# Float32 values without zero columns, weight chunks decoded in halves behind the heads, three query buffers and 20 constant products, in a windowed-attention and feed-forward kernel

## The chip, the cores and the metric

The kernel runs on one core of a Trainium2 chip. The metric is the device time of one execution in microseconds, as the median of several runs. The core has a matrix engine (TensorE, PE in the rows, with PEld for its weight loads), a vector engine (VectorE, DVE), a scalar engine (ScalarE, ACT), a general engine (GpSimd, POOL) and a queue engine that issues most DMAs (SyncE, SP; SPq is its instruction queue). Each engine works through its own instructions in a fixed order.

## The reference

There are 8 batches of 8 heads. Each head has 512 local tokens and 32 global ones, of 64 elements. A local query sees the 32 global keys and the local keys at most 32 positions away; a global query sees all keys. The attention's output, 4608 rows of 512, goes through a feed-forward layer of width 2048.

```python
s_g   = scale * q_g @ k_all.T;          out_g = softmax(s_g) @ v_all
s_ll  = where(abs(i - j) <= 32, scale * q_l @ k_l.T, -1e9)
a_l   = softmax(concat([scale * q_l @ k_g.T, s_ll]));   out_l = a_l @ v_all
x = concat([out_g, out_l]) as (4608, 512)
h = x @ w_in;  r = maximum(h, 0);  g = s * (r * r) + b;  out = g @ w_out
```

## The kernel before, in words

The work of a head is cut into two halves of 256 queries; one such half is called a head here, counted by `j` from 0 to 127. Eight heads (`j` = 8t to 8t+7) give one tile of 256 rows of x, and tile t of the feed-forward layer is worked in eight steps `m` = 8t to 8t+7, each with 24 products into `ps_h` (L517) and 12 into `acc` (L549). A 17th tile holds the global rows. Most operands are held as two parts, a rounded one and its remainder, so that the products are accurate; but the first NF = 16 heads use plain float32 operands, as their splitting would add to the start.

The loop over `j` (L602) traces, in this order: the loads of head j+2, the loads of weight chunks, the decoding of weight chunk `j` (only for j below 16), the scores of head `j`, the feed-forward step m = j - 10, the transposes of head j-1, the product with the values of head j-2 (`pv32`, L332, which works on two heads together when the second is due), the load of values, the split of a finished x tile (`x_split`, L484, at j = 9, 17, ...), and the second half of feed-forward step m-1.

**Weight chunks.** The weights of the feed-forward layer come as 16 chunks of 1 MB (`weight_load`, L139), each in two loads into a staging buffer. `weight_words` (L154) decodes a chunk into `w_all` with three ScalarE instructions (L160, L161, L168) and three VectorE instructions (L164, L165, L169), each over 1024 columns; the first two chunks (BY_HALVES = 2) are decoded in two halves of 512 columns. Step m needs chunks 2m and 2m+1. The staging buffers are those of the x tiles (xs0, xs1) and of the split queries and keys (kq).

**Float32 heads.** `load32` (L261) loads the queries `rq`, with zeros in the rows of the pair's other head, into one of two buffers in turn: the only `rq` buffer, or `tg`. `v_load32` (L274) loads values from `in_vz`, 192 KB a head: beside the head's 64 columns stand 64 columns of zeros, so that both heads of a pair add into the same 128 rows of `ps_o`. There are two `rv` buffers. `scores32` (L279) makes four constant products (`keep_busy`, L102) while j is below 10, then the scores, and for every second head the products of the global queries (L295); `softmax` (L217) has VectorE and ScalarE by turns.

**Order.** The instructions get a rank as they are traced. A planner hands each engine, at each step of its own estimate of time, the ready instruction that ranks first, and gives out buffers in the same way; so the order on each engine is fixed when the program is built. The functions of the first 16 heads are traced under

```python
with tc.high_priority(offset=AHEAD):
```

which ranks them AHEAD places earlier. AHEAD is 0. A DMA that needs a buffer waits in the SP queue for it, and what is behind it in that queue waits too. The 28 constant products at the start (WARM_FIRST, L107) give TensorE work while the first loads come. The loads of the scalars s and b (L566, L567) are the first two on the SP queue.

Of the kernel before, what the change touches and what calls it, by code (L numbers as in the profile page):

```python
# [10 lines left out]
F32 = mybir.dt.float32  # L11
# [9 lines left out]
B, H, SL, SG, D = 8, 8, 512, 32, 64  # L21
DM, DF = 512, 2048
P = 128
HALF = 256
# [16 lines left out]


NF = 16
AHEAD = 0


LAG = 10
SPLIT_AT = {8 * t + 9: t for t in range(16)}
WARM_UNTIL = 10
WARM_FIRST = 28  # L50
WARM_HEAD = 4

SPOTS = ["xs0", "xs1", "kq", "kq"] * 2 + ["xs1", "kq", "kq"] * 2 + ["xs1", "kq"]
LOADS_AT = {0: (0, 1), 1: (2, 3), **{j: (j + 2,) for j in range(2, 14)}}
BY_HALVES = 2
NORM_ACT = lambda j: j < 0
X_ACT = lambda j: j >= 8
G_AT = (13, 18)
# [9 lines left out]


@with_exitstack  # L70
def window_attention_then_ffn(ctx: ExitStack, tc: tile.TileContext, qd, qg, kw, vw, vg, qz, qgz, vz, w_in, w_out, sv, bv, out):
    nc = tc.nc
    scale = 1.0 / math.sqrt(D)

# [11 lines left out]
    sb = ctx.enter_context(tc.tile_pool(name="sb", bufs=2))  # L86
# [7 lines left out]
    s_t = const.tile([P, 1], F32, name="s_t")  # L94
    b_t = const.tile([P, 1], F32, name="b_t")
# [6 lines left out]
    def keep_busy(n, name):  # L102
        p_w = ps.tile([P, 512], F32, tag="acc1", name=name)
        for _ in range(n):
            nc.tensor.matmul(p_w, lhsT=warm[:, 0:P], rhs=warm, start=True, stop=True)

    keep_busy(WARM_FIRST, "warm0")  # L107


    for tile_, c0, shift in ((mask_low, 32, -32), (mask_mid, 32, 0), (mask_high, 0, 32)):  # L110
        nc.gpsimd.memset(tile_, 0.0)
        part = tile_[:, c0:c0 + 192]
        for sign, base in ((1, -shift), (-1, 64 + shift)):
            nc.gpsimd.affine_select(
                out=part, in_=part, pattern=[[sign, 192]], compare_op=ALU.is_ge,
# [23 lines left out]
    def weight_load(k):  # L139
        st = ops.tile([P, 2048], I32, tag=SPOTS[k], name=f"wst{k}", bufs=1 + (SPOTS[k] == "kq"))  # L140
        staged[k] = st
        sources = (w_in[k], w_out[k * P:(k + 1) * P, :])
        for i in range(2):
            queue = nc.scalar if k == 0 else nc.sync
            queue.dma_start(st[:, 1024 * i:1024 * (i + 1)], sources[i])

    def weight_chunk(k):
        st = staged.pop(k)
        n = 2 if k < BY_HALVES else 1
        for i in range(n):  # L150
            c = 1024 // n
            weight_words(k, st[:, 2 * c * i:2 * c * (i + 1)], slice(c * i, c * (i + 1)))

    def weight_words(k, st, at):  # L154
        words = st.rearrange("p (n w) -> p n w", w=2)
        low, high = words[:, :, 0], words[:, :, 1]
        n = at.stop - at.start
        pool, tag = ((ops, "vsg"), (sb, "pg"))[(k + at.start // 512) % 2]
        up = pool.tile([P, n], I32, tag=tag, name=f"wup{k}_{at.start}", bufs=1)
        nc.scalar.activation(out=up, in_=low.bitcast(U32), func=AF.Copy, scale=2.0**-29)  # L160
        nc.scalar.activation(  # L161
            out=low.bitcast(F32), in_=high.bitcast(F32), func=AF.Prelu, scale=2.0**-112, alpha=2.0**32,
        )
        nc.vector.tensor_scalar(out=low, in0=low, scalar1=3, scalar2=None, op0=ALU.logical_shift_left)  # L164
        nc.vector.tensor_tensor(out=low, in0=low, in1=up, op=ALU.add)  # L165
        m = low.bitcast(F32)
        hi, lo = (w_all[:, i, k].rearrange("p w c -> p (w c)")[:, at] for i in range(2))
        nc.scalar.copy(out=hi, in_=m)  # L168
        nc.vector.tensor_sub(out=lo, in0=m, in1=f32(hi))  # L169
# [3 lines left out]
    st_ = {}  # L173

    def slot(j):
        return j // 16, (j // 8) % 2, j % 8

    def load(j):
        b, hf, h = slot(j)
        if h % 2 == 0:  # L180
            rk = sb.tile([P, NK], F32, tag="rk", name=f"rk{j}", bufs=2)
            nc.sync.dma_start(rk, kw[b, hf, h // 2])
            st_["rk", j] = st_["rk", j + 1] = rk
        rq = sb.tile([P, HALF], F32, tag="rq", name=f"rq{j}", bufs=1)
        nc.sync.dma_start(rq, qd[b, hf, h])
        st_["rq", j] = rq

    def v_load(j):
        b, hf, h = slot(j)
        rv = sb.tile([P, 6 * D], F32, tag="rv", name=f"rv{j}")[:, 0:3 * D]  # L190
        nc.sync.dma_start(rv, vw[b, hf, h])
        st_["rv", j] = rv

# [60 lines left out]
    def x_tile(j):  # L254
        b, hf, h = slot(j)
        t = 2 * b + hf
        if h == 0:
            xcur[t] = sb.tile([P, 4, HALF], F32, tag="x", name=f"x{t}", bufs=1)
        return xcur[t]

    def load32(j):  # L261
        b, hf, h = slot(j)
        if h % 2 == 0:
            rk = sb.tile([P, NK], F32, tag="rk", name=f"rk{j}", bufs=2)
            nc.sync.dma_start(rk, kw[b, hf, h // 2])
            st_["rk", j] = st_["rk", j + 1] = rk
        if j % 2 == 0:
            rq = sb.tile([P, HALF], F32, tag="rq", name=f"rq{j}", bufs=1)
        else:
            rq = sb.tile([P, 288], F32, tag="tg", name=f"rq{j}", bufs=1)[:, 0:HALF]  # L270
        nc.sync.dma_start(rq, qz[j])
        st_["rq", j] = rq

    def v_load32(j):  # L274
        rv = sb.tile([P, 6 * D], F32, tag="rv", name=f"rv{j}")
        nc.sync.dma_start(rv, vz[j])
        st_["rv", j] = rv

    def scores32(j):  # L279
        b, hf, h = slot(j)  # L280
# [35 lines left out]
    def pieces(hf):  # L316
        q0 = MIDQ[hf][0]
        yield 0, P, slice(0, P), slice(0, P)
        yield 2, P, slice(NP - P, NP), slice(P, 2 * P)
        yield 1, MID, slice(P, NP - P), slice(q0, q0 + NP - 2 * P)  # L320
# [11 lines left out]
    def pv32(j):  # L332
        b, hf, h = slot(j)
        x = x_tile(j)
        if h % 2 == 0:
            return
        p_o = ps.tile([P, 2 * P], F32, tag="o", name=f"ps_o{j}")
        for i in (j - 1, j):
            pt, rv = st_.pop(("pt", i)), st_.pop(("rv", i))
            for c, n, o, q in pieces(hf):  # L340
                nc.tensor.matmul(  # L341
                    p_o[:, q], lhsT=rv[0:n, c * P:(c + 1) * P], rhs=pt[0:n, o],
                    start=(i < j and c == 0), stop=(i == j and c == 1),
                )
        x_out = x[:, h // 2, :]
        if X_ACT(j):
            nc.scalar.copy(out=x_out, in_=p_o)
        else:
            nc.vector.tensor_copy(out=x_out, in_=p_o)

    def qg_load(b):
        rqg = sb.tile([P, H * SG], F32, tag="xr", name=f"rqg{b}", bufs=1)
        nc.sync.dma_start(rqg, qgz[0] if b == 0 else qg[b])
        st_["rqg", b] = rqg

    def qg_load32(b):
        n = min(NF - 16 * b, H) * SG
        rqg = ops.tile([P, n], F32, tag="u", name=f"rqw{b}", bufs=1)
        nc.sync.dma_start(rqg, qgz[b, :, 0:n])
        st_["rqg", b] = rqg  # L360
# [202 lines left out]
                    rows = out.rearrange("(b r) d -> r b d", r=SL + SG)[16 * i:16 * i + 16, :, :]  # L563
                    nc.sync.dma_start(rows, o)

    nc.sync.dma_start(s_t, sv.partition_broadcast(P))  # L566
    nc.sync.dma_start(b_t, bv.partition_broadcast(P))  # L567

    NM = NT * 8
    extra, early, late = defaultdict(list), {}, {}  # L570
    for b in range(B):
# [10 lines left out]
    def pick(f32_one, split_one):  # L582
        def run(j):
            if NF <= j < NS:
                split_one(j)
            elif 0 <= j < NF:
                with tc.high_priority(offset=AHEAD):
                    f32_one(j)
        return run
# [5 lines left out]
    tr = pick(transposes32, lambda j: None)  # L595
    vsp = pick(lambda j: None, v_split)
    pvs = pick(pv32, lambda j: None)
    piece, last = 0, None
    qg_load(0)
    ld(0)  # L600
    ld(1)
    for j in range(NM + LAG + 2):  # L602
        sp(j + 1)
        ld(j + 2)
        vl(j)
        for k in LOADS_AT.get(j, ()):
            weight_load(k)
        if j < 16:
            weight_chunk(j)
            piece += 1  # L610
        if j < NS:
            b1 = j // 16 + 1
            if j == 14 and NF > 16:
                qg_load32(1)
            elif j % 16 == 14 and b1 < B:
                qg_load(b1)
            sc(j)
            if j == NF - 1 and NF % 16:
                if NF > 16:
                    qg_load(j // 16)  # L620
                qg_split(j // 16)
            if j % 16 == 15 and NF <= j + 1 < NS:
                qg_split(b1)
        if j in early:
            early.pop(j)()
        m = j - LAG if LAG <= j < NM + LAG else None
        if m is not None:
            ffn_in(m)
            if m == 8 * 15 + 7:
                xg_split(16)  # L630
        tr(j - 1)
        transposes_and_pv(j - 1, j - 2)
        vsp(j - 1)
        for fn in extra.pop(j, []):
            fn()
        pvs(j - 2)
        vl32(j)
        if j in SPLIT_AT:
            x_split(SPLIT_AT[j])
        if last is not None:  # L640
            ffn_out(last)
        last = m
        if j in late:
            late.pop(j)()
# [73 lines left out]
```

## Time and profile before

| | |
|---|---|
| median of 3 runs | 1037.92 us (1036.88 to 1038.34) |
| the profiled execution | 1040.1 us, span 1038.3 us |
| TensorE busy | 1008.4 us, 97% |
| VectorE busy | 793.1 us, 76% |
| ScalarE busy | 709.5 us, 68% |
| GpSimd busy | 282.1 us, 27% |
| moved by DMA | 82.05 MB |

The median is the time to compare with. The span is that of the instructions in the profiled execution, which was 1.8 us longer as a whole, and rows of the trace give times from the span's start. An engine is busy while it has an instruction in work. The constant products count as busy time of TensorE, though nothing reads them.

### The profile page before, as it was taken

To read this page: it belongs to the slowest core of one execution; us is meant where nothing else is said; L and a number is where in the kernel's file an instruction comes from. 1 tells how busy PE (TensorE), PEld (TensorE's weight loads), DVE (VectorE), ACT (ScalarE), POOL (GpSimd) and SP (SyncE) were. 2 spreads that over 40 slices of the span, in tenths; PEclk is the share of its full clock that TensorE was granted. 3 is DMA by queue.
4 is the path that set the end of the run, shared out by engine and by line. 5 is a ranking of instruction groups with operands and counts; after the bars stand their busy time and mean duration, and the time that the engine had idled before them with its cause. 6 is when DMAs were issued, how large, how long until landed. Compare 5 with 4: busy or idle time off the path is not lost.

```text
span 1038.3 us, 20034 instructions
## 1 busy us (share of the span) xinstructions
PE 1008.4 (97%) x6956; PEld 912.8 (88%) x6956; DVE 793.1 (76%) x2069; ACT 709.5 (68%) x1775; POOL 282.1 (27%) x366
## 2 busy tenths in 40 slices
PE   8669999999999999999999999999999999999998
PEld 4449999989999999999999999999999999999987
DVE  4888587788888888897779787898879787874322
ACT  6988576676777776786678686777678676754222
POOL 1001142333233242342243243332343233301000
PEclk9889999999999999999999999999999999999999
DMA  8774131321222121321123131222122122201000
GB/s 310 254 231 151 51 100 39 90 58 43 83 64 89 48 78 49 101 63 58 57 60 96 44 93 50 87 63 66 55 76 82 36 91 60 65 5 48 17 27 21
DMA packets 63558, 82.05 MB, mean 79 GB/s; under 512 B 7649, under 2 KB 50657, under 8 KB 63457
## 3 DMA queue, kind: packets, MB, share of 16 engines
q1 hardware_dynamic: 63168, 79.72, 25.0%
q8 instruction: 55, 0.90, 0.4%
q10 hardware_dynamic: 288, 1.05, 0.3%
q14 instruction: 47, 0.38, 0.1%
HBM read 71.30 MB, written 9.44 MB: 78 GB/s over the span
## 4 chain that ended last, share of the span: by engine, by line
PE 90%; DMA 3%; ACT 3%; DVE 3%; issue 1%; SPq 0%; DVEq 0%; ACTq 0%
PE ps_h L517 36%; PE acc L549 35%; PE ps_s L375 5%; PE ps_o L403 4%; PE turned L311 2%; PE turned L313 2%; PE ps_og L469 2%; PE ps_g L382 1%; DMA rk<-in_kw 1%; DMA wst<-in_w_in 1%; PE ps_o L341 1%; PE turned L447 1%; PE ps_s L286 1%; ACT wup L160 1%; ACT sm L231 1%
## 5 line engine op out<-in xcount | busy, mean ns | idle before, releaser
L517 PE MATMUL ps_h<-xst,w_all 128*128 128x256 f32 x3264 | 437.7, 281 | 2.7 <-ACT xst L489 1.8
L549 PE MATMUL acc<-w_all,g 128*128 128x512 f32 x1632 | 419.5, 396 | 0.0
L517 PEld LDWEIGHTS ps_h<-xst,w_all 128*128 128x128 f32 x3264 | 407.9, 189 | 10.0 <-ACT xst L489 2.0
L549 PEld LDWEIGHTS acc<-w_all,g 128*128 128x128 f32 x1632 | 291.2, 188 | 51.0
L231 ACT ACTIVATE sm<-sm,nm 128x224 f32<-128x224 f32 x256 | 121.5, 477 | 45.5 <-DVE nm L225 43.8
L524 DVE SCALAR_TENSOR_TENSOR r<-ps_h,s_t,r 128x512 f32<-128x512 f32 x136 | 101.4, 746 | 63.2 <-ACT r L523 62.2
L206 POOL TENSOR_TENSOR kq<-rq,kq 128x256 fp32r<-128x256 f32 x112 | 87.0, 777 | 203.1 <-ACT kq L205 188.5
L214 POOL TENSOR_TENSOR vs<-rv,vs 128x192 fp32r<-128x192 f32 x112 | 70.7, 631 | 259.9 <-ACT vs L213 253.6
L532 DVE SCALAR_TENSOR_TENSOR g<-r,b_t,g 128x512 fp32r<-128x512 f32 x136 | 108.4, 797 | 36.2 <-ACT g L531 32.3
L523 ACT ACTIVATE r<-ps_h 128x512 f32<-128x512 f32 x136 | 81.2, 597 | 75.3 <-PE ps_h L517 68.3
L531 ACT ACTIVATE g<-r,b_t 128x512 fp32r<-128x512 f32 x136 | 98.5, 724 | 37.4 <-DVE r L524 35.4
L241 DVE TENSOR_SCALAR sm<-sm,nm 128x224 f32<-128x224 f32 x256 | 83.1, 366 | 4.0
L461 POOL TENSOR_TENSOR vsg<-rvg,vsg 128x320 fp32r<-128x320 f32 x64 | 56.9, 911 | 105.2 <-ACT vsg L460 105.1
L375 PE MATMUL ps_s<-kq 128*128 128x224 f32 x448 | 75.0, 277 | 0.0
L375 PEld LDWEIGHTS ps_s<-kq 128*128 128x128 f32 x448 | 67.3, 190 | 6.4
L311 PE MATMUL turned<-ident,sm 128*96 128x128 f32 (+1 forms) x256 | 64.6, 277 | 6.3 <-DVE sm L241 6.3
L392 ACT CAST pt<-turned 128x416 fp32r<-128x416 f32 x112 | 57.5, 513 | 15.4 <-PE turned L313 14.5
L393 DVE TENSOR_TENSOR pt<-turned,pt 128x416 fp32r<-128x416 f32 x112 | 65.2, 583 | 2.8 <-ACT pt L392 2.0
L387 DVE TENSOR_TENSOR sg<-ps_g,tg 32x256 f32<-32x256 f32 (+1 forms) x112 | 48.2, 430 | 23.4 <-ACT tg L386 19.3
L403 PE MATMUL ps_o<-pt,vs 128*128 128x256 f32 x336 | 64.0, 296 | 0.1
L313 PE MATMUL turned<-ident,sm 128*128 128x128 f32 x256 | 63.8, 275 | 0.0
L204 POOL TENSOR_TENSOR kq<-rk,kq 64x352 fp32r<-64x352 f32 x56 | 60.2, 1074 | 10.5 <-ACT kq L203 5.1
(79 smaller groups left out, 1267.2 us busy)
## 6 DMA issues: line engine op xcount, KB each, us to landing
rq<-in_qd SPq DMA_DIRECT2D x112, 128.0 KB, 2.0
rk<-in_kw SPq DMA_DIRECT2D x64, 176.0 KB, 2.3
rv<-in_vw SPq DMA_DIRECT2D x112, 96.0 KB, 1.9
rvg<-in_vg SPq DMA_DIRECT2D x32, 320.0 KB, 3.0
out<-o SPq DMA_DIRECT2D x34, 256.0 KB, 2.1
wst<-in_w_in SPq DMA_DIRECT2D x15, 512.0 KB, 4.8
wst<-in_w_out SPq DMA_DIRECT2D x15, 512.0 KB, 5.7
rv<-in_vz SPq DMA_DIRECT2D x16, 192.0 KB, 3.5
```

The costliest lines, as they stand in the source:

```text
L206: nc.gpsimd.tensor_sub(out=qs[:, 1, :], in0=rq, in1=f32(qs[:, 0, :]))
L231: nc.scalar.activation(out=p, in_=p, func=AF.Exp, bias=nm[:, blk:blk + 1], scale=-1.0, accum_out=ss[:, blk:blk + 1],)
L241: nc.vector.tensor_scalar(out=p, in0=p, scalar1=ss[:, blk:blk + 1], scalar2=1.0, op0=ALU.mult, op1=ALU.mult,)
L311: nc.tensor.transpose(out=p_t[0:n, s0:s0 + P], in_=sm[:, c0:c0 + n], identity=ident)
L313: nc.tensor.transpose(out=p_t[:, o0:o0 + P], in_=sm[:, c0:c0 + P], identity=ident)
L375: nc.tensor.matmul(p_s[:, W * blk:W * blk + W], lhsT=qs[:, a, blk * P:(blk + 1) * P], rhs=ks[:, KEYS[blk]], start=(a == 0), stop=(a == 1),)
L403: nc.tensor.matmul(p_o[:, :, q], lhsT=vs[0:n, c], rhs=pt[0:n, :, o], start=(c == 0), stop=(c == 1))
L517: nc.tensor.matmul(p_h[:, k], lhsT=wi[:, a, f, c], rhs=xs[:, e, c, :], start=(n == 0), stop=(n == 11),)
L524: nc.vector.scalar_tensor_tensor(out=r, in0=p_h, scalar=s_t, in1=r, op0=ALU.mult, op1=ALU.mult)
L531: nc.scalar.activation(out=g[:, 0], in_=r, func=AF.Identity, bias=b_t)
L532: nc.vector.scalar_tensor_tensor(out=g[:, 1], in0=r, scalar=b_t, in1=f32(g[:, 0]), op0=ALU.add, op1=ALU.subtract,)
L549: nc.tensor.matmul(oacc[t][i], lhsT=g[:, a, k, i * P:(i + 1) * P], rhs=wo[:, e, f, :], start=(pr == 0 and n == 0), stop=(pr == 7 and n == 5),)
```

## The change

Values: `vz` is gone. The first 16 heads load their values as all others do (`v_load`, 96 KB), into one of three `rv` buffers of half the size. `pv32` multiplies with 64 stationary columns and writes the 64 rows of `ps_o` that belong to the head, each head with its own start and stop. Queries: `rq` has two buffers, and the float32 heads go through three in turn (`rq`, `rq`, `tg`). Chunks: all 16 are decoded in halves, so every chunk takes six ScalarE and six VectorE instructions of 512 columns; the traced place of loads and decodings stays but for chunk 2, which is loaded at j = 0. Order: the functions of the first 16 heads rank 50 places earlier. Start: 20 constant products in place of 28, and the loads of s and b are traced at j = 3.

```diff
-AHEAD = 0
+AHEAD = 50
-WARM_FIRST = 28
+WARM_FIRST = 20
-LOADS_AT = {0: (0, 1), 1: (2, 3), **{j: (j + 2,) for j in range(2, 14)}}
-BY_HALVES = 2
+DECODED_AT = [0, 1, 2, 3, 4, 5, 6, 7, 8, 9, 10, 11, 12, 13, 14, 15]
+BY_HALVES = 16
...
-        rq = sb.tile([P, HALF], F32, tag="rq", name=f"rq{j}", bufs=1)
+        rq = sb.tile([P, HALF], F32, tag="rq", name=f"rq{j}", bufs=2)
...
-        rv = sb.tile([P, 6 * D], F32, tag="rv", name=f"rv{j}")[:, 0:3 * D]
+        rv = sb.tile([P, 3 * D], F32, tag="rv", name=f"rv{j}", bufs=3)
...
-        if j % 2 == 0:
-            rq = sb.tile([P, HALF], F32, tag="rq", name=f"rq{j}", bufs=1)
+        if j % 3 < 2:
+            rq = sb.tile([P, HALF], F32, tag="rq", name=f"rq{j}", bufs=2)
...
     def v_load32(j):
-        rv = sb.tile([P, 6 * D], F32, tag="rv", name=f"rv{j}")
-        nc.sync.dma_start(rv, vz[j])
-        st_["rv", j] = rv
+        v_load(j)
...
             for c, n, o, q in pieces(hf):
+                d0 = D * (i % 2)
                 nc.tensor.matmul(
-                    p_o[:, q], lhsT=rv[0:n, c * P:(c + 1) * P], rhs=pt[0:n, o],
-                    start=(i < j and c == 0), stop=(i == j and c == 1),
+                    p_o[d0:d0 + D, q], lhsT=rv[0:n, c * D:(c + 1) * D], rhs=pt[0:n, o], start=(c == 0), stop=(c == 1),
                 )
...
-    nc.sync.dma_start(s_t, sv.partition_broadcast(P))
-    nc.sync.dma_start(b_t, bv.partition_broadcast(P))
...
     for j in range(NM + LAG + 2):
+        if j == 3:
+            nc.sync.dma_start(s_t, sv.partition_broadcast(P))
+            nc.sync.dma_start(b_t, bv.partition_broadcast(P))
         sp(j + 1)
         ld(j + 2)
         vl(j)
-        for k in LOADS_AT.get(j, ()):
-            weight_load(k)
-        if j < 16:
-            weight_chunk(j)
+        while loaded < 16 and (loaded < 2 or DECODED_AT[loaded] <= j + 2):
+            weight_load(loaded)
+            loaded += 1
+        while piece < 16 and DECODED_AT[piece] <= j:
+            weight_chunk(piece)
             piece += 1
```

## Rows read from the trace of the kernel before

**Rows 1.** Stages: length, busy PE, PEld, DVE, ACT, POOL, PE clock, DMA share, GB/s.

```profile
0.00:10.36 10.36, 8.91 (x28) 3.31 (x28) 1.61 (x3) 4.16 (x7) 3.19 (x15) 1.00 0.59 202
10.36:80.89 70.53, 49.31 (x223) 33.45 (x223) 57.51 (x146) 61.43 (x110) 0.00 (x0) 0.86 0.80 273
80.89:119.40 38.51, 38.51 (x261) 35.60 (x260) 29.18 (x67) 27.89 (x62) 8.64 (x9) 0.98 0.35 109
119.40:1000.00 880.60, 878.00 (x6244) 810.53 (x6243) 695.98 (x1844) 607.50 (x1586) 270.25 (x342) 1.00 0.22 63
```

**Rows 2.** Timeline of PE: start, length, instruction; idle time before it and what ended it.

```profile
14.80 0.65 PE L295 MATMUL ps_g<-rk,rqg 128*64 128x256 f32 x2 [1.97 <-ACT sg L300]
15.38 1.02 PE L286 MATMUL ps_s<-rk,rq 128*128 128x224 f32 x4
...
39.58 1.70 PE L286 MATMUL ps_s<-rk,rq 128*128 128x224 f32 x4
...
54.66 0.99 PE L295 MATMUL ps_g<-rk,rqg 128*64 128x288 f32 x2 [2.56 <-DMA rk<-in_kw]
...
65.84 0.47 PE L311 MATMUL turned<-ident,sm 128*128 128x128 f32 x1 [3.44 <-DVE sm L241]
...
74.27 0.89 PE L341 MATMUL ps_o<-pt,rv 128*128 128x128 f32 x6
...
80.89 4.92 PE L517 MATMUL ps_h<-xst,w_all 128*128 128x256 f32 x34
```

**Rows 3.** Timeline of ACT and DVE at the end of the start.

```profile
71.82 1.14 ACT L160 ACTIVATE wup<-wst 128x1024 int32<-128x1024 uint32 x1 [0.64 <-DMA wst<-in_w_out]
...
73.33 0.42 DVE L349 COPY x<-ps_o 128x256 f32<-128x256 f32 x1
...
76.29 0.61 ACT L489 CAST xst<-x 128x512 fp32r<-128x512 f32 x1
```

**Rows 4.** What the SP queue waited for from 10.36 to 80.89: total, times, longest.

```profile
SPq L276 <- PE ps_o L341: 18.0, 10, 5.6
SPq L271 <- PE ps_s L286: 9.3, 9, 2.3
SPq L145 <- DVE w_all L169: 8.7, 5, 4.7
```

**Rows 5.** ACT in the same stretch by line and shape: busy, mean ns, idle before.

```profile
L160 ACT ACTIVATE wup<-wst 128x1024 int32<-128x1024 uint32 x12 | 13.7, 1151 | 4.6 <-DMA wst<-in_w_out 4.6
L168 ACT CAST w_all<-wst 128x1024 fp32r<-128x1024 f32 x11 | 12.5, 1133 | 0.6 <-DVE wst L165 0.5
...
L168 ACT CAST w_all<-wst 128x512 fp32r<-128x512 f32 x4 | 2.7, 666 | 0.7 <-DVE wst L165 0.7
...
L160 ACT ACTIVATE wup<-wst 128x512 int32<-128x512 uint32 x2 | 1.3, 660 | 1.6 <-DMA wst<-in_w_in 1.6
```

**Rows 6.** DVE in the same stretch by line and shape, one kind.

```profile
L165 DVE CUSTOM_DVE_ANT_0 wst<-wst,wup 128x2048 uint16<-128x2048 uint16 x11 | 13.4, 1221 | 0.1
...
L165 DVE CUSTOM_DVE_ANT_0 wst<-wst,wup 128x1024 uint16<-128x1024 uint16 x3 | 2.1, 690 | 0.1
```

**Rows 7.** The same columns, from 10.36 to the second cast of x.

```profile
10.36:76.30 65.94, 45.71 (x209) 30.61 (x208) 53.42 (x135) 56.89 (x104) 0.00 (x0) 0.87 0.81 278
```

**Rows 8.** PE among the first constant products: length, busy, clock, DMA share, GB/s.

```profile
6.00:7.00 1.00, 1.00 (x4) 1.00 0.90 360
7.00:8.00 1.00, 1.00 (x6) 1.00 1.04 377
```

**Rows 9.** First issues of the SP queue: start, length.

```profile
0.74 0.40 SPq L566 DMA_DIRECT2D s_t<-in_sv  x1
1.20 0.41 SPq L567 DMA_DIRECT2D b_t<-in_bv  x1
```

**Rows 10.** Loads of values in the first 150 us: count, KB each, median us to landing.

```profile
rv<-in_vz SPq DMA_DIRECT2D x16, 192.0 KB, 3.5
...
rv<-in_vw SPq DMA_DIRECT2D x6, 96.0 KB, 1.8
```

More of the change, by code (lines that the diff above doesn't have):

```diff
@@ L70, in window_attention_then_ffn @@
 @with_exitstack
-def window_attention_then_ffn(ctx: ExitStack, tc: tile.TileContext, qd, qg, kw, vw, vg, qz, qgz, vz, w_in, w_out, sv, bv, out):
+def window_attention_then_ffn(ctx: ExitStack, tc: tile.TileContext, qd, qg, kw, vw, vg, qz, qgz, w_in, w_out, sv, bv, out):
     nc = tc.nc
@@ L597, in window_attention_then_ffn @@
     pvs = pick(pv32, lambda j: None)
-    piece, last = 0, None
+    piece, loaded, last = 0, 0, None
     qg_load(0)
@@ L688 @@
     qz, qgz = qd.reshape(-1, 2, P, HALF)[0:NF // 2].copy(), qg[0:2].reshape(2, P, H // 2, 2, SG).copy()
-    vz = _np.zeros((NF // 2, 2, P, 3, 2, D), dt)
     for i in range(2):
@@ L693 @@
         qgz[:, other, :, i] = 0
-        vz[:, i, :, :, i] = vw.reshape(-1, 2, P, 3, D)[0:NF // 2, i]
-    qz, qgz, vz = qz.reshape(NF, P, HALF), qgz.reshape(2, P, H * SG), vz.reshape(NF, P, 6 * D)
+    qz, qgz = qz.reshape(NF, P, HALF), qgz.reshape(2, P, H * SG)
     w_in = a["moe_w_in"].reshape(DM // P, P, DF // P, P).transpose(2, 1, 0, 3)
@@ L702 @@
     ins = {
-        "qd": qd, "qg": qg, "kw": kw, "vw": vw, "vg": vg, "qz": qz, "qgz": qgz, "vz": vz, "w_in": w_in, "w_out": w_out,
+        "qd": qd, "qg": qg, "kw": kw, "vw": vw, "vg": vg, "qz": qz, "qgz": qgz, "w_in": w_in, "w_out": w_out,
         "sv": a["moe_s"], "bv": a["moe_b"],
@@ L711 @@
     args.append(nc.dram_tensor("out_0", (B * (SL + SG), DM), F32, kind="ExternalOutput").ap())
-    for i in (8, 9):
+    for i in (7, 8):
         args[i] = args[i].bitcast(I32)
```

## The prediction

> **What bounds the kernel now.** I first read the busy time by stage. From 119.4 to 1000 us TensorE is busy in 878.0 of 880.6 us at a granted clock of 1.00 [rows 1]; that stretch is set by the number of products, and the change takes none of them away. So I look for its effect ahead of that. From 80.9 to 119.4 us TensorE has no idle time either. From 10.4 to 80.9 us it is busy in 49.3 of 70.5 us, and part of that is constant products and products at a clock of 0.86 [rows 1]. What the kernel loses, it loses before 80.9 us.
>
> The timeline of TensorE says what it lacks there: it waits for softmax (3.44 us ahead of 65.84) and for a load of keys (2.56 us ahead of 54.66), and only at 80.89 does the feed-forward layer come in force, 34 products at once [rows 2]. From then on there is always such work. The reader is to see what that moment hangs on: the last values of heads 6 and 7 are copied into x at 73.33, ScalarE casts the second half of x at 76.29, and ahead of the cast it has already taken up the thirteenth chunk (number 12) at 71.82 [rows 3]. In traced order the cast stands behind chunk 9; the heads have thus fallen about 3.7 chunks behind. Up to the cast ScalarE is the fullest engine of those that feed TensorE, 56.9 of 65.9 us, before VectorE with 53.4 [rows 7].
>
> Last, the waits of the SP queue: 18.0 us for `rv` buffers, 9.3 for `rq` buffers and 8.7 for staging buffers of chunks [rows 4]. What stands behind the first two in the queue, keys and chunks, goes out late: ScalarE waits 4.6 and 1.6 us for chunks' second and first loads in this stretch [rows 5].
>
> **The change part by part.** The sum counts in time to the cast of x, as what follows shifts with it.
>
> *Chunks in halves.* In rows of ScalarE a whole instruction takes 1151 ns (L160) or 1133 (L168), a half 660 or 666 [rows 5]. L161 has the shape and kind of L160 and is taken as its equal. A chunk costs 2 x 1151 + 1133 = 3.44 us whole and 4 x 660 + 2 x 666 = 3.97 in halves: 0.53 us more, for 14 chunks 7.4. If neighbours overlapped fully at their ends it would be nothing; I take 0.53, as a row gives it. VectorE pays alike: 2 x 690 - 1221 = 159 ns for one of three pairs [rows 6], some 0.48 a chunk; it is the less full and is not in the sum. If it became the fuller, its 0.48 would take the place of the 0.53.
>
> *Heads ranked 50 places earlier.* An iteration traces about 40 instructions once chunks have twelve, so 50 places are about 1.25 chunks. With the waits below, I take it that the heads make up 2.7 of their 3.7 chunks, so that the cast comes with chunk 10; the bounds are 0 (the heads were late because they were not ready, and rank helps no instruction that isn't) and 4.
>
> *Buffers of values and queries, values without zeros.* Three buffers each let a load go out one head earlier, and a load of values is 96 KB rather than 192, with medians of 1.8 and 3.5 us to landing [rows 10]. The 27.3 us of SP waits for `rv` and `rq` should shrink, and with them the loads of keys and chunks behind. On the path this is worth what ScalarE idles for: 65.9 - 56.9 = 9.0 us [rows 7], of which 6.2 are for chunks [rows 5]. I take half of the 6.2, so about 6.0 us of idle time stay; the bounds are 9.0 and 3. In the long middle the extra buffers are worth nothing, for TensorE doesn't wait there [rows 1].
>
> *64 stationary columns.* As many products, with the same moving columns, so nothing; six passes take 0.89 us a head [rows 2], hidden in a stretch with 21 us of idle TensorE. Were they to cost half as much again, sixteen heads would add 7 us of products, mostly in that idle time.
>
> *Start.* The two loads that go to later held the SP queue for 2 x 0.46 us [rows 9], so the first keys can come 0.9 us earlier. The constant products run at 4, later 6 in a microsecond [rows 8]; eight fewer free TensorE 1.3 to 2 us earlier. The first head gains the smaller, 0.9 us; the bounds are 0 and 2. At j = 3 the scalars wait among other loads, and nothing needs them before the feed-forward layer.
>
> *Sum.* Up to the cast before: 10.7 whole chunks' worth of instructions (36.8 us), 5.3 us of halves, 14.8 us of heads and the like (56.9 less these), 9.0 idle: 65.9. After: 10.7 - 2.7 = 8.0 chunks x 3.97 = 31.8, 5.3, 14.8 and 6.0 idle make 57.9, so 8.0 us earlier. About one head's products fewer are then done (1.02 for the scores, 0.89 for the values [rows 2]), 2 us to be done later. With 0.9 from the start the gain is 6.9.
>
> *Given back later.* From 80.9 to 119.4 us ScalarE had 27.9 us of work in 38.5 [rows 1]. Now 2.7 chunks more come into it (10.7 us) and the last 3 cost 1.6 more: 40.2. That doesn't fit, but chunk 15 is needed only by step 7 of the first tile, and the chunks left over can slip past the stretch. I take 1.4 us of new TensorE waits; the bounds are 0 and 7.2 (below). Gain 5.5 us: the profiled execution would go from 1040.1 to 1034.6. It lies 2.2 above the median shown, so the forecast for the median is 1037.9 - 5.5 = 1032.4 us.
>
> **The rivals.** *More (0.20).* The heads make up 4 chunks and ScalarE idles 3 us: 6.7 x 3.97 + 20.1 + 3 = 49.7, 16.2 earlier, less 4 for two heads and 3 for waits, plus 0.9: 10 us, 1028; with halves that cost nothing 3.6 more, 1024. For it speaks that so much of the delay is in waits for buffers that now exist; against it that ScalarE would be 94% busy.
>
> *Slower (0.17).* Heads stay as far behind, since they wait for each other (one buffer for the scores, one for the transposes) and not for their turn; the halves are then pure cost on ScalarE: 10.7 x 3.97 + 20.1 + 9.0 = 71.6, 5.7 later, 4.8 with the start: 1042.7. It decides when the heads make up less than 5.7 / 3.97 = 1.4 chunks. The long waits for softmax [rows 2] speak for it, the many SP waits [rows 4] against.
>
> *Nothing (0.14).* The cast comes earlier, but ScalarE is then the bound: at the 86% that it reached before the cast [rows 7] it does 33.1 of the 40.2 us in that stretch, and 7.1 us are given back: 1038. TensorE's freedom from waits from 80.9 on [rows 1] came with ScalarE at 72%.
>
> *Clock (0.05).* With fewer constant products the first two heads run at the lower clock: scores 1.70 for 1.02 us [rows 2], so some 4 us over two heads' chain, hence 1036.4. Against it: after 1.97 us without work the products at 15.38 still took 1.02 [rows 2], and I expect a gap of at most 1.1 us. The Trainium skill (TensorE: Matmul & The Clock Gate, What's actually happening) says that the lower clock is the default and work lifts it; by that rule shorter work at the start can only hurt, which the rows here don't show for so short a gap.
>
> **How the numbers follow.** The forecast's own case has 0.44, from 1028 to 1036 (idle time 3 to 9, waits 0 to 4). A measurement can tell 0.2%, 2.1 us, from no change. The likeliest case, but for 0.01, and "more" are faster: 0.63. "Nothing", "clock" and that 0.01 are within: 0.20. "Slower" is 0.17. The range takes in most of "more" and of "slower": 1022 to 1042.5, leaving out about 0.07 below and 0.10 above.
>
> **What would show it.** The second cast of x (L489) near 68 us with chunk 10 begun, and not 12, ahead of it; SP waits for `rv` and `rq` well under 27 us; TensorE full from about 73 us with under 2 us of idle time before 115. If the cast is early and TensorE waits for L523, L531 or a decoded chunk after it, "nothing" is right; if 12 chunks still stand before the cast, "slower". The prediction is wrong if the planner's new order changes TensorE's waits in the long middle, of which no row here tells.

## The result and the profile after

The changed kernel takes 1023.03 us (median of 4 runs, 1022.68 to 1025.52), against 1037.4 for the kernel before beside it: a ratio of 0.9874, interval 0.9844 to 0.9904. That is 14.4 us; 5.5 were forecast.

Its stages, as in [rows 1] (length, busy time of PE, PEld, DVE, ACT, POOL, clock, DMA share, GB/s), and below them the stretch up to its cast of x, as in [rows 7]:

```profile
0.00:8.10 8.10, 6.65 (x20) 2.55 (x21) 1.47 (x3) 3.19 (x5) 3.19 (x15) 1.00 0.75 251
8.10:51.20 43.10, 38.22 (x210) 25.22 (x211) 37.68 (x133) 40.66 (x104) 0.00 (x0) 1.00 0.75 259
51.20:90.00 38.80, 38.80 (x244) 33.05 (x245) 34.41 (x95) 35.18 (x79) 1.34 (x2) 1.00 0.58 192
90.00:110.00 20.00, 14.67 (x81) 12.10 (x80) 16.39 (x34) 17.85 (x36) 3.50 (x4) 0.88 0.48 170
110.00:1000.00 890.00, 888.09 (x6303) 819.34 (x6302) 714.69 (x1844) 606.32 (x1590) 281.52 (x345) 1.00 0.21 63
...
10.36:47.69 37.33, 33.41 (x183) 21.96 (x184) 32.66 (x117) 35.83 (x92) 0.00 (x0) 1.00 0.79 280
```

The start is 30 us shorter: the feed-forward layer comes in force at 51.2, not at 80.9 [rows 1, 2], and the granted clock of TensorE stays at 1.00 where it was 0.86. ScalarE is busy in 35.8 of the 37.3 us ahead of the cast, 96%, where it had 86% [rows 7]. But half of the 30 us is lost again, and two rows say where. From 90 to 110 us TensorE is busy in 14.7 of 20 us, at a granted clock of 0.88. And from 51.2 to 90 it is "busy" throughout, but with 244 products in 38.8 us, where it had 261 of much the same kinds in 38.5 [rows 1].

The cast itself, in the timeline of ScalarE, as in [rows 3]:

```profile
47.13 0.67 ACT L160 ACTIVATE wup<-wst 128x512 int32<-128x512 uint32 x1
47.69 0.62 ACT L487 CAST xst<-x 128x512 fp32r<-128x512 f32 x1
```

It is the fourteenth L160 of a half: seven chunks have been taken up ahead of the cast, not thirteen. The timeline of TensorE, as in [rows 2], with the first product of a head, the coming of the feed-forward layer, and the stops from 90 us on:

```profile
8.10 0.93 PE L284 MATMUL ps_s<-rk,rq 128*128 128x224 f32 x4
...
51.20 2.78 PE L515 MATMUL ps_h<-xst,w_all 128*128 128x256 f32 x22
...
95.62 0.50 PE L515 MATMUL ps_h<-xst,w_all 128*128 128x256 f32 x2 [1.72 <-ACT w_all L168]
...
103.39 0.34 PE L373 MATMUL ps_s<-kq 128*128 128x224 f32 x1 [0.99 <-DVE kq L204]
...
106.22 1.17 PE L373 MATMUL ps_s<-kq 128*128 128x224 f32 x4 [1.74 <-DVE nm L225]
```

At 95.62 it waits for a decoded chunk, then for splits and softmax behind chunks on ScalarE and VectorE. The waits of the SP queue from 10.36 to 51.2, as in [rows 4]:

```profile
SPq L191 <- PE ps_o L340: 5.3, 6, 2.0
SPq L265 <- PE ps_s L284: 5.1, 4, 2.5
SPq L271 <- PE ps_s L284: 4.3, 3, 3.3
```

Those for value and query buffers (L191 and L271), 27.3 us before, are 9.6. The halves of chunks, from 8.1 to 51.2, as in [rows 5], last 684 ns (L160) and 665 (L168), much as the rows of before had them:

```profile
L160 ACT ACTIVATE wup<-wst 128x512 int32<-128x512 uint32 x13 | 8.9, 684 | 1.0 <-DMA wst<-in_w_out 0.7 <-DMA wst<-in_w_in 0.3
...
L168 ACT CAST w_all<-wst 128x512 fp32r<-128x512 f32 x13 | 8.6, 665 | 0.0
```

### The profile page after: what moved, and what is told of

Read it like the earlier page. It is cut to its first block, busy times and chain, and to the rows that moved or that the text cites. A ratio compares the mean times of both kernels' runs of the same rounds, so it can differ in the third digit from the quotient of the medians.

```text
span 1021.1 us, 20069 instructions
## 1 busy us (share of the span) xinstructions
PE 1002.6 (98%) x6946; PEld 906.3 (89%) x6948; DVE 809.2 (79%) x2111; ACT 708.1 (69%) x1817; POOL 289.5 (28%) x366
## 4 chain that ended last, share of the span: by engine, by line
PE 90%; DVE 4%; DMA 3%; ACT 2%; issue 1%; SPq 0%; POOL 0%; ACTq 0%; DVEq 0%
PE ps_h L515 35%; PE acc L547 35%; PE ps_s L373 4%; PE ps_o L401 4%; PE turned L309 2%; PE turned L311 2%; PE ps_og L467 2%; PE ps_g L380 1%; DMA rk<-in_kw 1%; PE ps_o L340 1%; PE ps_s L284 1%; PE turned L445 1%; DMA wst<-in_w_in 1%; DMA wst<-in_w_out 1%; DMA rv<-in_vw 1%
## 5 line engine op out<-in xcount | busy, mean ns | idle before, releaser
L231 ACT ACTIVATE sm<-sm,nm 128x224 f32<-128x224 f32 x256 | 121.7, 478 | 35.8 <-DVE nm L225 34.6
L530 DVE SCALAR_TENSOR_TENSOR g<-r,b_t,g 128x512 fp32r<-128x512 f32 x136 | 111.8, 822 | 34.8 <-ACT g L529 30.4
L206 POOL TENSOR_TENSOR kq<-rq,kq 128x256 fp32r<-128x256 f32 x112 | 92.2, 823 | 146.9 <-ACT kq L205 138.6
L241 DVE TENSOR_SCALAR sm<-sm,nm 128x224 f32<-128x224 f32 x256 | 93.4, 406 | 4.0
L385 DVE TENSOR_TENSOR sg<-ps_g,tg 32x256 f32<-32x256 f32 (+1 forms) x112 | 48.2, 430 | 23.4 <-ACT tg L384 18.1
L384 ACT COPY tg<-ps_g 32x256 f32<-32x256 f32 (+1 forms) x112 | 42.2, 377 | 32.0 <-PE ps_g L380 29.5
```

Source lines behind the costliest of these rows:

```text
L206: nc.gpsimd.tensor_sub(out=qs[:, 1, :], in0=rq, in1=f32(qs[:, 0, :]))
L231: nc.scalar.activation(out=p, in_=p, func=AF.Exp, bias=nm[:, blk:blk + 1], scale=-1.0, accum_out=ss[:, blk:blk + 1],)
L241: nc.vector.tensor_scalar(out=p, in0=p, scalar1=ss[:, blk:blk + 1], scalar2=1.0, op0=ALU.mult, op1=ALU.mult,)
L530: nc.vector.scalar_tensor_tensor(out=g[:, 1], in0=r, scalar=b_t, in1=f32(g[:, 0]), op0=ALU.add, op1=ALU.subtract,)
```

## The experiments

**One part undone.** Three runs take back the rank, the halves or the third query buffer; a fourth takes the values alone into the kernel before. The number of chunks taken up ahead of the second cast is read from each program's order on ScalarE.

```diff
# a_rank0, on the changed kernel
-AHEAD = 50
+AHEAD = 0
# a_whole, on the changed kernel
-BY_HALVES = 16
+BY_HALVES = 2
# a_q2, on the changed kernel
...
-        if j % 3 < 2:
-            rq = sb.tile([P, HALF], F32, tag="rq", name=f"rq{j}", bufs=2)
+        if j % 2 == 0:
+            rq = sb.tile([P, HALF], F32, tag="rq", name=f"rq{j}", bufs=1)
# b_val, on the kernel before
-        rv = sb.tile([P, 6 * D], F32, tag="rv", name=f"rv{j}")[:, 0:3 * D]
+        rv = sb.tile([P, 3 * D], F32, tag="rv", name=f"rv{j}", bufs=3)
...
-                    p_o[:, q], lhsT=rv[0:n, c * P:(c + 1) * P], rhs=pt[0:n, o],
+                    p_o[d0:d0 + D, q], lhsT=rv[0:n, c * D:(c + 1) * D], rhs=pt[0:n, o], start=(c == 0), stop=(c == 1),
```

> The changed kernel with the float32 heads at their own rank (AHEAD 0). In its program 8 chunks are taken up ahead of the second cast of x, against 7 in the changed kernel and 13 in the one before. Order theory: the 14.4 us come from the 6 chunks that now stand behind the cast, 2.4 us each, so 1025.4 us. Buffer theory: what counts is that loads no longer wait in the SP queue, so rank gives nothing, 1023. If rank were the main part: over 1031.

Measured: 1021.61 us, ratio 0.9852 (0.9815 to 0.9889).

> The changed kernel with chunks 2 to 15 decoded whole. 9 chunks are taken up ahead of the second cast. Order theory: two chunks more in front of it, 1027.8 us. ScalarE theory: after the cast ScalarE is the bound and the halves cost it 7.4 us there and before, so whole chunks are faster, 1016 to 1020. Buffer theory: no change, 1023.

Measured: 1022.32 us, 0.9861 (0.9825 to 0.9897).

> The changed kernel with the two query buffers of before (rq and tg in turn). 9 chunks are taken up ahead of the second cast. Order theory: 1027.8 us. Buffer theory: the waits of the SP queue for query buffers come back (9.3 us before) and most of the gain goes, 1032 or more. If a third buffer is worth nothing: 1023.

Measured: 1024.58 us, 0.988 (0.9843 to 0.9918).

> The kernel before with the values alone changed: no zeros, 96 KB a head, 64 stationary columns, three value buffers. 13 chunks are taken up ahead of the second cast, as before. Order theory: no change, 1037. Buffer theory: the 18.0 us of SP waits for value buffers shrink and chunks and keys come earlier, 1031 or less.

Measured: 1041.95 us, 1.0058 (1.0037 to 1.0079).

None of the three parts is missed: each may go, and a gain of 12 to 15 us stays (14.4 with all of them). The order theory's 2.4 us a chunk falls with a_rank0 and a_whole, and the ScalarE theory with a_whole; the buffer theory falls with a_q2. And the values alone are no gain but by the medians a loss, although the cast there came at 70.15 us rather than 76.29. The runs of b_val spread over 9 us, and they go with the clock that each was granted on average: 1038.6 us at 0.990, the most, and 1047.6 at 0.980, the least. Four executions of the kernel before at 0.990, taken beside it, took 1033.4 to 1037.7 us. So at the same clock 1 to 5 us of the loss are left, by a single execution of b_val.

**One part alone, and ScalarE relieved.** If any part may go, the question is which suffices.

```diff
# b_half, on the kernel before
-BY_HALVES = 2
+BY_HALVES = 16
# b_q3, on the kernel before
...
-        if j % 2 == 0:
-            rq = sb.tile([P, HALF], F32, tag="rq", name=f"rq{j}", bufs=1)
+        if j % 3 < 2:
+            rq = sb.tile([P, HALF], F32, tag="rq", name=f"rq{j}", bufs=2)
# b_rank50, on the kernel before
-AHEAD = 0
+AHEAD = 50
# a_pool, on the changed kernel
-        nc.scalar.copy(out=hi, in_=m)
+        (nc.gpsimd.tensor_copy if k >= 4 else nc.scalar.copy)(out=hi, in_=m)
```

> The kernel before with all chunks in halves, alone. 10 chunks are taken up ahead of the second cast of x (13 before). Ceiling theory: the cast at some 62 us (4.8 us a chunk, from the casts of the changed kernel and the one before), and the time falls with the cast until a ceiling of about 1021 is met: 1024. Rival, the parts add up: a third of the gain, 1032. Rival, halves only cost ScalarE: 1042.

Measured: 1023.5 us, 0.9868 (0.985 to 0.9885).

> The kernel before with three query buffers, alone. 11 chunks are taken up ahead of the second cast. Ceiling theory: cast at some 66 us, 1027. Parts add up: 1032. If the buffers alone do nothing without the rank: 1037.

Measured: 1031.49 us, 0.9944 (0.9926 to 0.9962).

> The kernel before with the float32 heads ranked 50 places earlier, alone. 11 chunks are taken up ahead of the second cast. Ceiling theory: as for three query buffers, 1027. Parts add up: 1032. If rank helps no instruction that isn't ready: 1037.

Measured: 1031.79 us, 0.9948 (0.9932 to 0.9963).

> The changed kernel with the rounding of chunks 4 to 15 (L168) on GpSimd, which has no work there; ScalarE is relieved of 24 halves of 0.67 us, 16 us. If ScalarE is the ceiling behind the cast: 1010 to 1016. If the ceiling is the loads of chunks or VectorE, or GpSimd is much slower at it: 1021 to 1026.

Measured: 1022.72 us, 0.9855 (0.9834 to 0.9875).

The halves alone are worth 13.0 us, nearly as much as the whole change; query buffers or rank alone are worth 5.0 and 4.7. In the trace of b_half the cast comes at 58.76, 17.5 us earlier than before. ScalarE's timeline there, with the cast directly behind a half, which starts 0.57 us ahead of it:

```profile
57.63 0.66 ACT L168 CAST w_all<-wst 128x512 fp32r<-128x512 f32 x1
58.19 0.67 ACT L160 ACTIVATE wup<-wst 128x512 int32<-128x512 uint32 x1
58.76 0.61 ACT L489 CAST xst<-x 128x512 fp32r<-128x512 f32 x1
```

a_pool took 24 halves from ScalarE and gained nothing. From 50 to 80 us VectorE became the full engine there (DVE 30.00 of 30.00, third of the busy times):

```profile
50.00:80.00 30.00, 29.84 (x191) 25.45 (x190) 30.00 (x75) 24.01 (x52) 8.54 (x11) 1.00 0.62 195
```

Its subtractions (L169) took 786 ns from 40 to 90 us, against 705 in the changed kernel, where GpSimd had next to nothing to do in that time; that the one comes of the other is not shown. So this run doesn't tell whether decoding is a ceiling, only that moving one step to GpSimd doesn't lift one.

**The stationary columns.** The timelines of TensorE showed something that the busy time hides. In a_rank0, 64 stationary columns (start, length):

```profile
74.31 0.49 PE L547 MATMUL acc<-w_all,g 128*128 128x512 f32 x1
74.74 0.43 PE L340 MATMUL ps_o<-pt,rv 128*64 128x128 f32 x2
75.10 0.49 PE L547 MATMUL acc<-w_all,g 128*128 128x512 f32 x1
75.53 0.43 PE L340 MATMUL ps_o<-pt,rv 128*64 128x128 f32 x2
75.89 0.49 PE L547 MATMUL acc<-w_all,g 128*128 128x512 f32 x1
```

and a place of the same kind with 128 stationary columns, in the run a_rank0_zeros below:

```profile
73.08 0.48 PE L549 MATMUL acc<-w_all,g 128*128 128x512 f32 x1
73.39 0.38 PE L341 MATMUL ps_o<-pt,rv 128*128 128x128 f32 x2
73.53 0.48 PE L549 MATMUL acc<-w_all,g 128*128 128x512 f32 x1
```

From start to start, a product into `acc` and two passes into `ps_o` take 0.43 + 0.36 = 0.79 us with 64 columns and 0.31 + 0.14 = 0.45 with 128: 0.34 us for each such place. The Trainium skill (TensorEngine Tiling (Array Packing), Key Properties) says that a change of tiling mode drains TensorE; these two timelines agree, at 0.34 us for going in and out. But 64 columns do not always bring a pause. Later in the kernel 112 products into `ps_g` and 320 into `ps_og` have 64 stationary columns too, but rounded operands, and among other products of rounded operands they show none; in a_rank0_zeros:

```profile
364.94 0.40 PE L549 MATMUL acc<-w_all,g 128*128 128x512 f32 x1
365.17 0.28 PE L382 MATMUL ps_g<-kq,qgs 128*64 128x256 f32 x1
365.29 2.66 PE L549 MATMUL acc<-w_all,g 128*128 128x512 f32 x11
```

Here the product into `acc` takes 0.23 us to the next start, and the one with 64 columns, which has half as many moving columns, takes 0.12. The pause is thus one of the plain float32 products; why they alone have it, no run shows. Three runs test what it costs, and one the decoding:

```diff
# a_zeros, on the changed kernel: values as in the kernel before (vz, 192 KB, two buffers)
...
     def v_load32(j):
-        v_load(j)
+        rv = sb.tile([P, 6 * D], F32, tag="rv", name=f"rv{j}")
+        nc.sync.dma_start(rv, vz[j])
+        st_["rv", j] = rv
...
-                    p_o[d0:d0 + D, q], lhsT=rv[0:n, c * D:(c + 1) * D], rhs=pt[0:n, o], start=(c == 0), stop=(c == 1),
+                    p_o[:, q], lhsT=rv[0:n, c * P:(c + 1) * P], rhs=pt[0:n, o],
+                    start=(i < j and c == 0), stop=(i == j and c == 1),
# a_rank0_zeros: the same, and
-AHEAD = 50
+AHEAD = 0
# a_zeros64: as a_zeros, but
...
+                    p_o[d0:d0 + D, q], lhsT=rv[0:n, c * P + d0:c * P + d0 + D], rhs=pt[0:n, o], start=(c == 0), stop=(c == 1),
# a_skip, on the changed kernel
+        m = high.bitcast(F32)
+        if k < 8:
             (L160, L161, L164, L165 as they were)
```

> The changed kernel with the values as before: zero columns, 192 KB a head, 128 stationary columns, two value buffers for the float32 heads. 8 chunks are taken up ahead of the second cast of x. Pause theory (a product with 64 stationary columns between products with 128 makes TensorE pause about 0.2 us each way, as start to start times around it show): 16 heads with 1 to 6 such places each give 4 to 8 us back, 1015 to 1019. Rival, the loads: values of 192 KB and one buffer less push the cast back by a chunk or two and nothing else happens, 1023 to 1028.

Measured: 1014.36 us, 0.9782 (0.9764 to 0.98).

> The same with the float32 heads at their own rank. 8 chunks ahead of the second cast. Pause theory: 1014 to 1018, below the run with rank 0 and 64 columns (1021.6). Rival, the loads: 1022 to 1028.

Measured: 1013.2 us, 0.9775 (0.9759 to 0.9792).

> The run with zero columns once more, with its 192 KB loads and two value buffers for the float32 heads, but with the head's own 64 columns as the stationary operand, written to the head's own 64 rows, as in the changed kernel. Only the number of stationary columns differs from that run (1014.4 us). Pause theory: the 8.7 us are lost again, 1021 to 1024. If loads or buffers made the difference: 1013 to 1016.

Measured: 1028.06 us, 0.9932 (0.9916 to 0.9948).

> The changed kernel without L160, L161, L164 and L165 for chunks 8 to 15, so that those chunks are only rounded and subtracted (their weights are not the right ones); ScalarE has some 21 us and VectorE some 18 us less to do. If the ceiling behind the cast is the decoding of chunks by ScalarE and VectorE together: 1005 to 1013. If it is the loads of chunks or TensorE's own pauses: 1018 to 1023.

Measured: 1013.57 us, 0.9779 (0.9762 to 0.9796).

All four lie outside what the theory that fits them had stated, by 0.6 to 4.1 us: the pause theory has the sign right and the size too small. a_zeros and a_zeros64 differ in nothing that is loaded or buffered. They differ in the stationary columns, with the rows written and each head's start and stop, and in what the planner makes of the order; 13.7 us lie between them. The changed kernel loses 8.7 us against a_zeros; that is what the columns cost less what the smaller loads and the third value buffer bring, for a_zeros64, which lacks these, takes 5.0 us more than the changed kernel (up to 3.3 of them by the clock, as worked out below). Both best kernels, a_zeros and a_rank0_zeros, beat the changed kernel as well as the one before.

The pauses account for a part of this. In the changed kernel the passes into `ps_o` stand in 20 groups among other products, 10 of them behind 51.2 us, where TensorE has little idle time to hide a pause in: at 0.34 us each 3.4 us, or at most 6.8 if all count. In a_zeros64 it is 24 groups, 14 of them behind 51 us: 4.8 to 8.2 us. A second part is the clock. The stretches in which TensorE was granted the lower of its two levels, 0.50 in the rows (columns as in [rows 1]), in a_zeros64:

```profile
39.10:42.52 3.42, 3.42 (x13) 2.85 (x12) 2.63 (x9) 3.19 (x8) 0.00 (x0) 0.50 0.23 67
52.76:56.17 3.41, 3.41 (x12) 2.64 (x13) 2.69 (x10) 3.00 (x8) 0.00 (x0) 0.50 0.08 15
110.78:117.61 6.83, 5.90 (x20) 5.22 (x21) 6.21 (x13) 5.32 (x13) 2.63 (x3) 0.50 0.09 26
```

and in a_zeros, where there is one:

```profile
108.98:112.40 3.42, 3.42 (x17) 3.32 (x16) 1.98 (x8) 2.10 (x6) 0.00 (x0) 0.50 0.38 107
```

What the lower level costs, two rows of a_zeros64 tell, ten products of one kind at either level:

```profile
104.70 1.34 PE L517 MATMUL ps_h<-xst,w_all 128*128 128x256 f32 x10
...
111.71 2.50 PE L517 MATMUL ps_h<-xst,w_all 128*128 128x256 f32 x10 [1.50 <-DVE w_all L169]
```

So 1.16 of 2.50 us, 46% of the busy time there, are the clock's doing: by this estimate up to 5.9 us in a_zeros64, 1.6 in a_zeros and 2.6 in the changed kernel (5.6 us of busy time, below). Pauses and clock together make 9 to 12 of the 13.7 us; the rest is not accounted for. a_rank0 and a_rank0_zeros, too, differ in the values alone. In neither did the clock fall in the first 1000 us of the profiled execution, and still 6.0 us lie between these executions (1019.93 and 1013.89) and 8.4 between the medians.

a_skip shows that decoding is a limit too: with it cut for eight chunks, the changed kernel gains 9.5 us, though its cast comes no earlier (48.05).

**The times against the cast.**

The second cast and the time at the lower clock (up to the first 150 us) are those of the profiled execution.

| kernel | columns | chunks ahead | second cast, us | median, us | profiled execution, us | of it TensorE busy at the lower clock, us |
|---|---|---|---|---|---|---|
| before | 128 | 13 | 76.29 | 1037.4 | 1040.1 | 18.1 |
| b_rank50 | 128 | 11 | 64.20 | 1031.79 | 1031.86 | 8.7 |
| b_q3 | 128 | 11 | 63.38 | 1031.49 | 1032.26 | 19.9 |
| b_half | 128 | 10 | 58.76 | 1023.5 | 1021.93 | 6.8 |
| a_rank0_zeros | 128 | 8 | 50.32 | 1013.2 | 1013.89 | 0 |
| a_zeros | 128 | 8 | 50.07 | 1014.36 | 1015.0 | 3.4 |
| b_val | 64 | 13 | 70.15 | 1041.95 | 1038.59 | 16.9 |
| a_q2 | 64 | 9 | 55.23 | 1024.58 | 1022.74 | 0 |
| a_whole | 64 | 9 | 53.81 | 1022.32 | 1021.96 | 0 |
| a_zeros64 | 64 | 7.5 | 49.18 | 1028.06 | 1028.27 | 12.7 |
| a_rank0 | 64 | 8 | 49.09 | 1021.61 | 1019.93 | 0 |
| after | 64 | 7 | 47.69 | 1023.03 | 1022.89 | 5.6 |
| a_pool | 64 | 7 | 46.92 | 1022.72 | 1023.46 | 3.4 |

With 128 columns the time falls as the cast comes earlier, by 23 to 24 us for 26 from end to end, though not evenly: the first 12 us bring some 6, the next 5 some 8. Not all of that is the cast. The kernel before ran at the lower clock in four stretches, of which TensorE was busy in 18.1 us:

```profile
34.39:41.22 6.83, 5.35 (x17) 3.94 (x18) 6.36 (x16) 6.78 (x15) 0.00 (x0) 0.50 0.45 166
54.87:58.28 3.41, 3.41 (x12) 2.59 (x11) 1.60 (x3) 3.36 (x7) 0.00 (x0) 0.50 0.17 68
65.11:71.94 6.83, 5.97 (x19) 4.09 (x20) 5.43 (x18) 4.91 (x10) 0.00 (x0) 0.50 0.73 238
78.76:82.17 3.41, 3.41 (x15) 3.27 (x14) 2.91 (x7) 3.36 (x8) 0.00 (x0) 0.50 0.91 339
```

and the changed kernel in one, behind TensorE's waits of 95 to 104 us:

```profile
105.17:112.00 6.83, 5.63 (x21) 4.98 (x21) 6.76 (x18) 5.37 (x13) 0.80 (x1) 0.50 0.20 58
```

At 46% of the busy time, up to 5.7 of the 17.2 us between these two executions are the clock, and up to 5.2 of the 18.2 between the kernel before and b_half. Whether a fuller TensorE keeps its clock because the heads come sooner, or the heads come sooner because it keeps its clock, no run separates. With the clock taken off in the same way, some 18 us are left for the 26 us of cast with 128 columns. With 64 columns and a cast from 46.9 to 55.2 us, all six kernels then lie at 1020 to 1023, wherever the cast is, and 6 to 9 us above the two with 128 columns and a cast at 50 us. So the ceiling of some 1021 us that I took from the first runs is one of the kernels with 64 columns; b_half, with 128, was near it with a cast that came later.

## Why the prediction was right, and where it was not

*What bounds the kernel* held: the gain lies ahead of the steady stretch, and with 128 columns it grows as the second cast of x comes earlier. In the changed kernel the first rows of output go out 12.2 us earlier than before, the next tile's 14.9, and the distance stays near 17 us to the end of the two profiled executions.

The median of 1023.0 lies in the range by 1 us, at its lower end. The forecast's own case, 1028 to 1036, did not come; it is nearest to the rival "more", with a chance of 0.20.

*Chunks in halves* is the step that failed. I had it as a cost on ScalarE of 0.53 us a chunk and nothing else; "slower" was built on it. The length of a half was right (684 and 665 ns), but neighbours overlap at their ends (the half at 47.13 us is 0.67 long, and the cast starts at 47.69). So ScalarE's busy time in a whole execution rose by 1.5 us from the kernel before to b_half (709.5 to 711.0) and by 4.4 from a_whole to the changed kernel (703.7 to 708.1), not by 7.4. And the sign of the whole was wrong: alone, the halves bring 13.0 us. In the order on ScalarE, 10 chunks rather than 13 then stand ahead of the cast, and ScalarE is fuller. Two reasons are argued and not told apart: a head's short instruction finds at most 0.7 us of a chunk in front of it, not 1.15; and the two `up` buffers hold two halves where they held two chunks, so decoding can't run as far ahead of the heads. The clock, which fell for a shorter time in b_half, may have a share of up to 5.2 us. I had priced the instructions and forgotten what waits behind one.

*Heads ranked earlier* was taken as the main part, with 2.7 chunks made up by rank and buffers, 4 at most; the whole change made up six. The 3.7 chunks that the heads were behind were one too many as well: at j = 9 chunks 0 to 9, ten of them, are traced ahead of the cast, and 12.7 stood there. Alone, rank makes up two and gives 4.7 us; undone, nothing is lost. The same holds for *three query buffers*, 5.0 us alone and some 2 when undone (12.3 us stay of 14.4). The parts overtake the same chunks and don't add up.

*The sum* had the cast 8 us earlier, with ten chunks taken up; it came 28.6 us earlier with seven. Its idle time, taken as 6.0 us, measured 1.5 (37.3 less 35.8).

*64 stationary columns* was the second step that failed: "as many products, so nothing" cost 8.7 us net of what the smaller loads bring (a_zeros), and 13.7 with the loads alike (a_zeros64). I had bounded it at 7 us, half a product's time, and put that into idle time; but 42 of the 96 passes stand behind 51.2 us, among products of the feed-forward layer, where TensorE has little idle time to hide a pause in.

*Given back later* was taken as 1.4 us of up to 7.2. TensorE's 5.3 us without work from 90 to 110 us are its visible part, and the pauses and the fall of the clock from 105.2 to 112.0 us its hidden ones. The rival "nothing" had the right place for the first, but not the size that decides.

*Start*: the first head's product into `ps_s` began at 8.10 us, 2.8 us earlier than before (10.94), not 0.9; with keys, queries and values now first in the SP queue, ahead of the global queries, the first head no longer began with L295. The clock didn't fall in the first 105 us. No run undoes the start alone, so its share of the gain is open.

So the median lay in the range because two errors went against each other: the cast moved more than three times as far as forecast, and about half of that was lost to causes of which one was counted too low and one not at all. That they met there was luck.

## What to carry to other kernels

Where several engines feed each other in a fixed order, the length of a filler instruction is a delay for whatever stands behind it: cutting it can be worth more than the fixed cost that the cut adds: here 13.0 us against 1.5 us of added ScalarE time. Judge a busy TensorE by its products in a microsecond, look at the clock that it was granted, and at the distance from start to start where products of different stationary width meet. When parts of a change all remove one obstacle, undo each and try each alone: here neither gave the value that the other did, and one part was a loss that the sum concealed.

## What the runs showed of the hardware that was not expected

Plain float32 products with 64 stationary columns among products with 128 cost 0.34 us a place on top of their own time (0.79 against 0.45 us from start to start), though PE counts as busy through it; products of rounded operands with 64 columns showed no such cost among others of rounded operands (0.12 us for 256 moving columns, 0.23 for 512 with 128 stationary ones). At the lower granted clock ten products took 2.50 us that took 1.34 at the higher one. VectorE's subtraction of 128 x 512 took 786 ns rather than 705 with GpSimd rounding beside it, and GpSimd took 833 ns, by a trace whose GpSimd times are rough, for a rounding that ScalarE does in 664.
